# Attention units in pairs, a wider weight decode and a new order of steps in a fused attention and MoE kernel

## The chip, the cores and the metric

One core of a Trainium2 chip runs the whole program. The metric is the device time of one execution in microseconds. Before the change it is 528.5 us, the median of three runs (527.78 to 528.66).

## The reference

Three stages follow each other, all in float32, with 1,152 tokens (2 batches of 576) and 8 heads of 64:

```python
scores = q @ k.T / 8                      # windowed: heads 0-3 plain (32 keys back),
scores = where(mask, scores, -1e9)        # heads 4-7 dilated (every 4th of 128 keys back)
attn = exp(scores - max); attn /= sum + 1e-9
x = (attn @ v)                            # as 1152 x 512
h = x @ w_in                              # 512 -> 1024, w_in in float64
solu = h * softmax(h)
ln = (solu - mean) / sqrt(var + 1e-6) * g_ln
x = ln @ w_out                            # 1024 -> 512, w_out in float64
for e in range(4):                        # all four experts, weighted
    out += p[:, e] * (relu(x @ w1[e]) @ w2[e])
```

## The kernel before

Attention is cut into twelve **units**: per batch three plain ones, P0 to P2 (192 queries of four heads), and three dilated ones, D0 to D2 (96 queries per head and phase). A unit (`att_U`) goes through the engines in this way. On TensorE (PE) a mask and 24 small matmuls write its scores (L266, L275) to a PSUM tile `pa`. VectorE (DVE) takes the maximum, subtracts it, and after the exp on ScalarE (ACT) takes the sum and its reciprocal (L296 to L305). A multiply by it (L307) runs on DVE or GpSimd (POOL). Then the unit is transposed, on PE with a copy to `pt` (L326), or, for the five units in `ASWAP`, by a DVE transposition and a way through DRAM (L312 to L320). PE multiplies with V (L337), and the result is split into a high part `xhi` and the rest `xlo` (L250).

All matmuls of the dense stages use a split of this kind: three matmuls (high x high, high x low, low x high) for one product. `conv_in` and `conv_out` decode the float64 weights with integer work on the raw words: two ACT instructions (L190, L192), a shift (L194), an "or" (L196) and an add (L198) on DVE or POOL, then the split into `wh` and `wl`. w_in comes in four tiles j=0 to 3 (VI), w_out in eight halves of 512 columns (VO.j.t).

`moe_H` multiplies a tile of 128 tokens with w_in (H.0 to H.8): 24 matmuls in blocks of six, one block for each j. Blocks 0 and 1 read the plain heads, 2 and 3 the dilated ones. It writes one of two PSUM buffers `pm`; then DVE takes the maximum (L372), ACT the exp, DVE the product with `e` (L376), and ACT or DVE normalises (L379, L381). `moe_T` brings a tile into transposed form `hh`, `hl`: T.0 to T.2 on PE, T.3 to T.8 through DRAM (a DVE transposition L414, a DMA to `dt` L422, one back to `et` L431). `moe_X` multiplies three columns of 384 tokens with w_out (X.c.0 and X.c.1, 48 matmuls each, L449), also into `pm`, and copies the result to `xf`. The expert stage follows with products in Strassen form (`up`, L562) and `down` (L634).

Schedule: the instructions of every engine run in the order in which the program issues them, and that order stands in the string `ORDER`. Each word runs a generator one step further, up to its next `yield`: `UP.0.0` is a step of unit P0 of batch 0, `H.1` one of `moe_H(1)`, `VO.1.0` one of `conv_out(1, 0)`. A word that begins with `l` issues a load on SyncE's (SP) DMA queue, `F.n` runs n warm-up matmuls on a constant (L86), and a `+` at the end moves the step's flexible instruction to another engine (`pick`, `copy`):

```python
for name in ORDER.split():
    alt[0] = name.endswith("+")
    if part[0] in single:
        single[part[0]](*args)
    else:
        gens.setdefault(name, makers[part[0]](*args)); next(gens[name], None)
```

## Time and profile before

| | us |
|---|---|
| median of three runs | 528.5 |
| the profiled execution's own time | 528.32 |
| its span, first to last instruction | 526.5 |
| PE busy | 513.6 (98%) |
| DVE busy | 356.4 (68%) |
| ACT busy | 190.6 (36%) |
| POOL busy | 186.7 (35%) |

Durations come from this one execution. A matmul's end is modelled, so PE's busy time is an upper bound on its work; where PE is shown as idle, it was. The chain that ended last is PE for 90% of the span. The instructions of one engine overlap a little at their ends, so the distance between two starts is shorter than the duration of one.

### The profile page before, as it was taken

Reading aid. Unit: us, or ns where it says so; the run is one execution under the profiler, and the core shown is the slowest. Engines: PE = TensorE matmul, PEld = TensorE weight load, DVE = VectorE, ACT = ScalarE, POOL = GpSimd, SP = SyncE. Lnnn points to the kernel's source line nnn. Section 1 sums busy time; section 2 is a strip of 40 time slices with the busy share of each in tenths; the row PEclk is TensorE's granted clock in tenths of the full one; section 3 lists DMA queues with packets and bytes.
Section 4 is the critical chain, followed back from the end, with each engine's and each line's share of the span. In section 5 each row is a group of like instructions: output and inputs, shape, how many; then the busy total and the mean of one; then the engine's idle time right before and its main releaser. Section 6 shows DMA issues by size and latency. Waiting matters only on the chain.

```text
span 526.5 us, 9419 instructions
## 1 busy us (share of the span) xinstructions
PE 513.6 (98%) x3971; PEld 457.9 (87%) x3971; DVE 356.4 (68%) x474; ACT 190.6 (36%) x294; POOL 186.7 (35%) x131
## 2 busy tenths in 40 slices
PE   7789999998999999999999999999999999999997
PEld 3568889888999999998989899898989989898986
DVE  7999898484999875754775485568448655853532
ACT  3766884363153422421422233142223213312200
POOL 3334321111345632830661273047117313820300
PEclk9999999999999999999999999999999999999999
...
GB/s 321 409 319 149 146 202 78 143 159 200 1 225 95 1 1 50 111 1 1 159 1 1 8 153 0 2 153 7 2 0 161 1 0 81 0 1 1 1 81 100
DMA packets 24490, 46.44 MB, mean 88 GB/s; under 512 B 4480, under 2 KB 9088, under 8 KB 24064
## 3 DMA queue, kind: packets, MB, share of 16 engines
q1 hardware_dynamic: 24448, 45.84, 25.4%
...
## 4 chain that ended last, share of the span: by engine, by line
PE 90%; DMA 4%; DVE 2%; ACT 1%; issue 1%; SPq 1%; ACTq 0%
PE pa L634 19%; PE pm L634 18%; PE pm L562 17%; PE pa L562 17%; PE pm L367 9%; PE pm L449 6%; DMA draw<-in_moe_w_in_dram 2%; PE pa L337 1%; DMA dt<-st 1%; DMA et<-dt 1%; PE pa L275 1%; PE pa L398 1%; SPq L151 0%; DVE hl L436 0%; ACT eva L192 0%
## 5 line engine op out<-in xcount | busy, mean ns | idle before, releaser
L575 DVE SCALAR_TENSOR_TENSOR hl<-ct,hh 128x512 fp32r<-128x512 f32 (+1 forms) x64 | 64.1, 1018 | 32.4 <-ACT hh L573 32.4
L573 ACT ACTIVATE hh<-ct 128x512 fp32r<-128x512 f32 (+1 forms) x64 | 42.2, 682 | 50.8 <-DVE ct L605 21.3
L634 PE MATMUL pa<-wl,hh 128*128 128x512 f32 (+1 forms) x148 | 57.3, 387 | 0.0
L634 PE MATMUL pa<-wh,hh 128*128 128x512 f32 (+1 forms) x148 | 57.2, 387 | 0.0
L634 PE MATMUL pa<-wh,hl 128*128 128x512 f32 (+1 forms) x148 | 57.1, 386 | 0.0
L562 PE MATMUL pm<-xoh,hl 128*128 128x256 f32 (+1 forms) x192 | 56.8, 296 | 0.0
L562 PE MATMUL pa<-xoh,hl 128*128 128x256 f32 (+1 forms) x192 | 56.8, 296 | 0.0
L562 PE MATMUL pm<-xol,hh 128*128 128x256 f32 (+1 forms) x192 | 56.8, 296 | 0.0
L562 PE MATMUL pa<-xol,hh 128*128 128x256 f32 (+1 forms) x192 | 56.8, 296 | 0.0
L562 PE MATMUL pm<-xoh,hh 128*128 128x256 f32 (+1 forms) x192 | 56.8, 296 | 0.0
L562 PE MATMUL pa<-xoh,hh 128*128 128x256 f32 (+1 forms) x192 | 56.8, 296 | 0.0
L634 PE MATMUL pm<-wl,hh 128*128 128x512 f32 (+1 forms) x144 | 55.7, 387 | 0.0
L634 PE MATMUL pm<-wh,hh 128*128 128x512 f32 (+1 forms) x144 | 55.7, 387 | 0.0
L634 PE MATMUL pm<-wh,hl 128*128 128x512 f32 (+1 forms) x144 | 55.6, 386 | 0.0
L481 POOL TENSOR_TENSOR wl<-wl,wh 128x1024 fp32r<-128x1024 f32 x7 | 16.9, 2413 | 94.7 <-ACT wh L176 94.7
L639 DVE SCALAR_TENSOR_TENSOR xf<-pm,pr,xf 128x512 f32<-128x512 f32 (+1 forms) x32 | 23.6, 738 | 31.1 <-PE pm L634 31.1
L639 DVE SCALAR_TENSOR_TENSOR xf<-pa,pr,xf 128x512 f32<-128x512 f32 (+1 forms) x32 | 23.6, 738 | 30.3 <-PE pa L634 30.3
L589 POOL TENSOR_TENSOR ct<-ct,ct 128x512 f32<-128x512 f32 (+1 forms) x16 | 24.1, 1506 | 54.3 <-ACT ct L587 54.3
L176 ACT CAST wh<-wl 128x1024 fp32r<-128x1024 f32 x16 | 16.8, 1052 | 70.3 <-PE pa L634 39.8
L481 POOL TENSOR_TENSOR hl<-sw,hh 128x512 fp32r<-128x512 f32 x20 | 29.4, 1475 | 28.2 <-ACT hh L176 28.2
L562 PEld LDWEIGHTS pm<-xoh,hh 128*128 128x128 f32 x192 | 36.4, 190 | 0.3
L562 PEld LDWEIGHTS pm<-xol,hh 128*128 128x128 f32 x192 | 36.4, 190 | 0.3
...
## 6 DMA issues: line engine op xcount, KB each, us to landing
wl<-in_moe_w_dram SPq DMA_DIRECT2D x16, 512.0 KB, 4.3
cvr<-in_moe_w_out_dram SPq DMA_DIRECT2D x8, 512.0 KB, 3.5
rw<-in_moe_w_dram SPq DMA_DIRECT2D x8, 512.0 KB, 4.9
wh<-in_moe_w_dram SPq DMA_DIRECT2D x8, 512.0 KB, 6.5
...
dt<-st SPq DMA_DIRECT2D x5, 512.0 KB, 3.0
...
```

Source lines behind the costliest of these rows:

```text
L176: nc.scalar.copy(out, in_)
L275: nc.tensor.matmul(ps[32 * g:32 * g + 32, j, 64 * m:64 * m + 64], lhsT=qt[rows, h, xq:xq + 32], rhs=kt[rows, h, xq:xq + 64], start=False, ...
L337: nc.tensor.matmul(po[64 * (g % 2):64 * (g % 2) + 64, j, o:o + 32], lhsT=vt[rows, m, g, :], rhs=pt[rows, m, g, :], start=True, stop=True)
L367: nc.tensor.matmul(pm[:, n, :], lhsT=xx[:, kk, cols], rhs=ww["in", kk][:, 512 * n:512 * n + 512], start=(n_ == 0 and i < 2), stop=(n_ == K ...
L449: nc.tensor.matmul(pm[:, dd, 0:CW], lhsT=w_, rhs=x_[:, f, :], start=(f == 0 and i == 0), stop=(f == KF - 1 and i == 2))
L481: pick().tensor_tensor(out=out, in0=a, in1=b, op=op)
L562: nc.tensor.matmul(ps[:, ff, 0:n], lhsT=a[:, kk, fc], rhs=b[:, kk, :], start=kk == 0 and m == 0, stop=kk == 1 and m == 2)
L573: nc.scalar.activation(out=hv, in_=src, func=AF.Relu)
L575: nc.vector.scalar_tensor_tensor(out=lv, in0=src, scalar=0.0, in1=hv.bitcast(F32), op0=ALU.max, op1=ALU.subtract)
L589: poolv().tensor_tensor(out=c12, in0=c21, in1=c22, op=ALU.add)
L634: nc.tensor.matmul(po[:, 0, 0:dn], lhsT=h_[:, f, cols], rhs=w_, start=(f == 0 and i == 0), stop=(f == 3 and i == 2))
L639: nc.vector.scalar_tensor_tensor(out=acc[:, t, dc], in0=po[:, 0, 0:dn], scalar=pr[:, t, e:e + 1], in1=acc[:, t, dc], op0=ALU.mult, op1=ALU ...
```

## The change

Batch 0 now has four attention units, `U.0.0` = P0, `U.1.0` = D0 and D1, `U.2.0` = P1, `U.3.0` = P2 and D2; batch 1 has three pairs. The units of a pair share the PSUM tiles, one maximum, subtraction, exp, sum, reciprocal, multiply and transposition copy. The multiply works in place in the `sm` tile, of which two (for four single units) take the place of three `sm` and three `pd` tiles. A POOL memset writes the constant 1e-9 that enters the sum. Two pairs of batch 1 (D0 and D1; P2 and D2) go through DRAM. `conv_out` decodes 1,024 columns at a time. `ORDER` is new from the first word up to the first steps of the expert stage; the loop over the experts behind it is as before.

```diff
-ASWAP = ("UD.0.1", "UD.1.1", "UD.2.1", "UP.1.1", "UP.2.1")
+PB = 2
+PAIRS = (((("P", 0),), (("D", 0), ("D", 1)), (("P", 1),), (("P", 2), ("D", 2))), ((("P", 0), ("P", 1)), (("D", 0), ("D", 1)), (("P", 2), ("D", 2))))
+ASWAP = ((1, 1), (2, 1))
 ORDER = """
-F.3 lP.0.0+ UP.0.0 lI.4 VI.4+ lD.0.0 VI.4 F.1 UP.0.0+ UP.0.0 lD.1.0+ VI.4 F.1 lP.1.0+ UD.0.0 UD.1.0 UP.0.0 VI.4 lI.0 UP.0.0+ VI.4 VI.0 lP.2.0 UD.0.0 UD.0.0+
...
+lD.0.0 lP.0.0+ F.10 lD.1.0+ F.4 lP.1.0+ U.0.0 lI.4 U.1.0 lP.2.0 U.0.0+ U.0.0 U.0.0 U.1.0 U.0.0+ U.2.0 lD.2.0+ U.0.0+ U.1.0 U.0.0+ F.1 U.1.0+ VI.4+ U.2.0 U.1.0+
...
-    pds = [ap1.tile([128, 3, 128], F32, name=f"pd{i}", tag=f"pd{i}") for i in range(3)]
-    sms = [ap1.tile([128, 6, 65], F32, name=f"sm{i}", tag=f"sm{i}") for i in range(3)]
+    sms = [ap1.tile([128, 6, 130], F32, name=f"sm{i}", tag=f"sm{i}") for i in range(PB)]
...
-    def conv_out(j, t):
-        sl = slice(512 * t, 512 * t + 512)
-        a = cva[:, sl]
-        yield from convert(cvr[:, 1024 * t:1024 * t + 1024], a)
...
+    def conv_out(j):
+        yield from convert(cvr, cva)
...
+        for t in range(2):
+            sl = slice(512 * t, 512 * t + 512)
+            hi, lo = whi["out", j][:, sl], wlo["out", j][:, sl]
+            gs = g_sb[:, 2 * j + t:2 * j + t + 1]
+            nc.scalar.activation(out=hi, in_=cva[:, sl], func=AF.Copy, scale=gs)
+            yield
+            nc.vector.scalar_tensor_tensor(out=lo, in0=cva[:, sl], scalar=gs, in1=hi.bitcast(F32), op0=ALU.mult, op1=ALU.subtract)
+            yield
...
+    def att_U(k, b):
+        us = PAIRS[b][k]
+        nu, n = len(us), sum(len(PAIRS[x]) for x in range(b)) + k
+        h0 = halves[k, b]
         ps = ptile(False)
...
+        nc_ = 3 * nu
+        swap = (k, b) in ASWAP
+        sb = sms[h0 // 2 % PB][:, 3 * (h0 % 2):3 * (h0 % 2) + nc_]
+        smx = sb.rearrange("p c (j k) -> p (c j) k", j=2)
...
+        nc.gpsimd.memset(sb[:, :, 65:66] if swap else sb[:, :, 129:130], 1e-9)
+        st = small.tile([128, 3, 12], F32, name="st", tag="st")[:, :, 0:2 * nc_]
+        sv = ps[:, :, 0:192 * nu].rearrange("p j (c k) -> p j c k", k=64)
+        nc.vector.tensor_reduce(out=st[:, 0].rearrange("p (j c) -> p j c", j=2), in_=sv, axis=AX.X, op=ALU.max)
+        yield
+        nc.vector.tensor_tensor(out=sm.rearrange("p c j k -> p j c k"), in0=sv,
+                                in1=st[:, 0].rearrange("p (j c) -> p j c", j=2).unsqueeze(3).to_broadcast([128, 2, nc_, 64]), op=ALU.subtract)
+        yield
+        se = smx[:, :, 1:65] if swap else sb[:, :, 1:129]
+        nc.scalar.activation(out=se, in_=se, func=AF.Exp, scale=SCALE)
+        yield
+        nc.vector.tensor_reduce(out=st[:, 1], in_=smx, axis=AX.X, op=ALU.add)
+        yield
+        nc.vector.reciprocal(out=st[:, 2], in_=st[:, 1])
+        yield
+        pick().tensor_tensor(out=sm, in0=sm, in1=st[:, 2].rearrange("p (c j) -> p c j", j=2).unsqueeze(3).to_broadcast([128, nc_, 2, 64]), op=ALU.mult)
+        yield
...
```

How the queues move, at three places.

DVE from the first scores on (`pa` holds scores, `sm` the softmax tile, `cva` the weight under decode). Before:

```order
L296 TENSOR_REDUCE st<-pa 128x6 [waits PE_49]
L298 TENSOR_TENSOR sm_131<-pa,st 128x6x64 [waits DVE_49]
L194 TENSOR_SCALAR cva<-cva 128x512 [waits Activation_49]
L196 SCALAR_TENSOR_TENSOR cva<-draw_196,cva 128x512 [waits DMAHW1_49,DVE_49]
L303 TENSOR_REDUCE st<-sm_131 128x6 [waits Activation_49]
L198 ISA cva<-draw_196,cva 128x1024 [waits DVE_49]
L296 TENSOR_REDUCE st<-pa 128x6 [waits PE_49]
```

And now:

```order
L292 TENSOR_REDUCE st<-pa 128x6 [waits PE_49]
L294 TENSOR_TENSOR sm_128<-pa,st 128x2x3x64 [waits DVE_49]
L300 TENSOR_REDUCE st<-sm_128 128x6 [waits Activation_49,Pool_49]
L302 RECIPROCAL st<-st 128x6 [waits DVE_49]
L292 TENSOR_REDUCE st<-pa 128x12 [waits PE_49]
L294 TENSOR_TENSOR sm_129<-pa,st 128x2x6x64 [waits DVE_49]
L292 TENSOR_REDUCE st<-pa 128x6 [waits PE_49]
L294 TENSOR_TENSOR sm_128<-pa,st 128x2x3x64 [waits DVE_49,PE_49,Pool_49]
L190 TENSOR_SCALAR cva<-cva 128x512 [waits Activation_49]
```

The sum of P0 now stands directly behind its subtraction, the pair D0 and D1 has one maximum of twelve columns, and the decode of w_in comes behind three units.

PE around the first block of H.0 (`wh_198`, `wh_302` are the high part of w_in's first tile). Before:

```order
L337 MATMUL pa<-pt,vp 64x32 [waits DMAHW2_49,Activation_49]
L337 MATMUL pa<-pt,vp 64x32 x23
L337 MATMUL pa<-pt,vd_117 64x32 [waits DMAHW3_49,Activation_49]
L337 MATMUL pa<-pt,vd_117 64x32 x23
L326 MATMUL pa<-ident,pd_128 128x128 [waits DVE_49,Pool_49]
L326 MATMUL pa<-ident,pd_128 128x128 x2
L367 MATMUL pm<-wh_198,xhi 128x512 [waits Activation_49]
```

And now:

```order
L278 MATMUL pa<-qkP_120 32x64 [waits DMAHW7_49]
L278 MATMUL pa<-qkP_120 32x64 x23
L372 MATMUL pm<-wh_302,xhi 128x512 [waits Activation_49]
L372 MATMUL pm<-wh_302,xhi 128x512
L372 MATMUL pm<-wl_303,xhi 128x512 [waits Pool_49]
L372 MATMUL pm<-wl_303,xhi 128x512 [waits DVE_49]
L372 MATMUL pm<-wh_302,xlo 128x512 x2
L323 MATMUL pa<-ident,sm_128 128x128 [waits DVE_49,PE_49]
```

The scores of the first two units of batch 1 (`qkP_120` is P1's) now stand ahead of H.0, and the block waits for POOL and DVE inside.

PE where X.0 ends (L449, L454) and the next H tile begins; the number at `pm` tells the tiles apart. Before, `pm_1370` is X.0.0 (X.0.1 was `pm_1345`) and `pm_1520` H.6:

```order
L449 MATMUL pm_1370<-hl_966,wh7_1424 128x384
L449 MATMUL pm_1370<-hh_965,wl7_1425 128x384
L367 MATMUL pm_1520<-wh0_198,xhi_90 128x512 [waits DVE_49,Activation_49]
L367 MATMUL pm_1520<-wh0_198,xhi_90 128x512
L367 MATMUL pm_1520<-wl0_199,xhi_90 128x512 x2
```

Now `pm_1364` is X.0.1 (X.0.0 is `pm_1415`) and `pm_1512` H.8:

```order
L454 MATMUL pm_1364<-hl_1007,wh7_1409 128x384
L454 MATMUL pm_1364<-hh_1006,wl7_1410 128x384
L372 MATMUL pm_1512<-wh0_302,xhi_90 128x512 [waits Activation_49]
L372 MATMUL pm_1512<-wh0_302,xhi_90 128x512
L372 MATMUL pm_1512<-wl0_303,xhi_90 128x512 x2
```

H.6 and H.7 have moved ahead of X.0, H.8 stands behind it, and of the two X.0 tiles the one that was begun first is now finished last.

## Rows read from the trace of the kernel before

**Rows 1.** Windows by stage: length, busy us (instructions) of each engine, PE clock, DMA.
```profile
0.00:40.50 40.50, 32.91 (x812) 21.47 (x812) 34.94 (x74) 24.56 (x39) 14.91 (x23) 1.00 0.89 341
...
44.70:111.60 66.90, 66.90 (x732) 57.97 (x730) 54.36 (x87) 44.63 (x71) 16.80 (x13) 1.00 0.49 151
111.60:131.00 19.40, 17.36 (x99) 16.62 (x97) 11.68 (x19) 8.00 (x13) 2.61 (x2) 1.00 0.60 179
...
165.00:522.00 357.00, 357.00 (x2079) 323.43 (x2078) 218.35 (x251) 98.70 (x151) 135.47 (x84) 1.00 0.12 40
```

**Rows 2.** Timeline of PE, waits behind the dense stretch: start, us, instruction, [idle before, releaser].
```profile
112.44 0.44 PE L449 MATMUL pm<-hl,wh 128*128 128x384 f32 x1 [0.65 <-POOL hl L436]
...
130.99 0.45 PE L449 MATMUL pm<-hl,wh 128*128 128x384 f32 x1 [0.80 <-DVE hl L436]
```

**Rows 3.** Chain that ended last: start, us; an X tile and twelve H blocks.
```profile
86.74 8.52 PE pm L449 x48
95.26 16.38 PE pm L367 x72
```

**Rows 4.** Timeline of DVE, two dense neighbours of 384 elements.
```profile
30.80 0.55 DVE L303 TENSOR_REDUCE st<-sm 128x6 f32<-128x390 f32 x1
31.27 0.55 DVE L296 TENSOR_REDUCE st<-pa 128x6 f32<-128x384 f32 x1
```

**Rows 5.** Groups by form, DVE, 0 to 45 us: busy us, mean ns, idle before.
```profile
L296 DVE TENSOR_REDUCE st<-pa 128x6 f32<-128x384 f32 x10 | 5.5, 552 | 1.6 <-PE pa L275 1.5
...
L194 DVE TENSOR_SCALAR eva<-eva 128x1024 uint32<-128x1024 uint32 x2 | 1.4, 688 | 0.2 <-ACT eva L192 0.2
...
L372 DVE TENSOR_REDUCE nmx<-pm 128x1 f32<-128x1024 f32 x1 | 1.2, 1224 | 0.3 <-PE pm L367 0.3
```

**Rows 6.** Timeline of PE: warm-ups (L86) and the first scores.
```profile
1.44 1.46 PE L86 MATMUL pm<-warm 128*128 128x512 bf16 x3 [1.44 <-DVE warm L81]
...
3.97 0.97 PE L275 MATMUL pa<-qkP 64*32 64x64 f32 x48
...
15.53 1.04 PE L86 MATMUL pm<-warm 128*128 128x512 bf16 x4
```

**Rows 7.** Timeline of DVE: first and last of five idle spots, 5 to 40 us.
```profile
6.39 0.43 DVE L194 TENSOR_SCALAR cva<-cva 128x512 uint32<-128x512 uint32 x1 [0.26 <-ACT cva L192]
...
28.59 0.69 DVE L194 TENSOR_SCALAR eva<-eva 128x1024 uint32<-128x1024 uint32 x1 [0.16 <-ACT eva L192]
```

**Rows 8.** Timeline of SP's DMA queue: issue of the 25th load.
```profile
27.84 0.33 SPq L151 DMA_DIRECT2D qkD<-in_qkd_dram  x1
```

**Rows 9.** Timeline of PE: the H block behind PE's last gap of the lead-in.
```profile
40.49 0.73 PE L367 MATMUL pm<-wh,xhi 128*128 128x512 f32 x2
```

**Rows 10.** Groups by form, ACT, 0 to 150 us: the copy of an X tile.
```profile
L176 ACT COPY xf<-pm 128x768 f32<-128x768 f32 x4 | 3.2, 801 | 18.0 <-PE pm L449 18.0
```

**Rows 11.** Timeline of DVE, ACT and SP: normalising on DVE; then the way of H.7.
```profile
104.54 0.75 DVE L381 TENSOR_SCALAR e<-e,nsum 128x1024 f32<-128x1024 f32 x1
...
111.66 1.23 DVE L372 TENSOR_REDUCE nmx<-pm 128x1 f32<-128x1024 f32 x1 [1.42 <-PE pm L367]
...
115.48 1.16 ACT L379 ACTIVATE e<-e,nsum 128x1024 f32<-128x1024 f32 x1 [0.26 <-DVE e L376]
...
117.23 1.24 DVE L414 STREAM_TRANSPOSE st<-e 128x1024 f32<-128x1024 f32 x1
...
118.62 0.60 SPq L422 DMA_DIRECT2D dt<-st  x1
```

**Rows 12.** Timeline of DVE and POOL: the add of half a tile, alone and beside POOL.
```profile
7.93 0.68 DVE L198 CUSTOM_DVE_ANT_0 cva<-draw,cva 128x1024 uint16<-128x1024 uint16 x1
...
82.72 1.68 DVE L198 CUSTOM_DVE_ANT_0 cva<-cvr,cva 128x1024 uint16<-128x1024 uint16 x1
...
82.21 1.64 POOL L198 TENSOR_TENSOR cva<-cva,cvr 128x512 uint32<-128x512 uint32 x1 [7.48 <-DVE cva L196]
```

**Rows 13.** DMA issues: KB each, median us to landing.
```profile
dt<-st SPq DMA_DIRECT2D x5, 512.0 KB, 3.0
```

More of the change, by code (lines that the diff above doesn't have):

```diff
@@ L324, in att_U @@
             tp = ptile(False)
-            for m in range(3):
-                nc.tensor.transpose(tp[:, 0, 128 * m:128 * m + 128], pd[:, m, :], ident)
+            for m in range(nc_):
+                o = 128 * (m % 3)
+                nc.tensor.transpose(tp[:, m // 3, o:o + 128], sb[:, m, 1:129], ident)
             yield
-            pt = ap2.tile([128, 3, 4, 32], F32, name="pt", tag="pt")
-            copy(pt.rearrange("p m g i -> p (m g i)"), tp[:, 0, 0:384])
+            pt = ap2.tile([128, 768], F32, name="pt", tag="pt")[:, 0:384 * nu].rearrange("p (m g i) -> p m g i", g=4, i=32)
@@ L330, in att_U @@
+            copy(pt.rearrange("p (u m) g i -> p u (m g i)", u=nu), tp[:, 0:nu, 0:384])
             yield
         po = ptile(False)
-        vt = vdt[b][t] if quad == "D" else vps.pop((t, b))
-        for m in range(3):
-            for g in range(4):
-                for j in range(2):
-                    rows, o = slice(64 * j, 64 * j + 64), 96 * (g // 2) + 32 * m
-                    nc.tensor.matmul(po[64 * (g % 2):64 * (g % 2) + 64, j, o:o + 32], lhsT=vt[rows, m, g, :], rhs=pt[rows, m, g, :],
-                                     start=True, stop=True)
@@ L339, in att_U @@
-        yield
-        segs = []
-        if quad == "P":
-            s0 = b * S + TH * t
-            segs.append((xhi[:, 0:2, s0:s0 + TH], xlo[:, 0:2, s0:s0 + TH], po[:, :, 0:TH]))
-        else:
-            ov = po[:, :, 0:TH].rearrange("p j (h x) -> p h j x", h=2)
-            x = 96 * t
-            while x < 96 * t + 96:
+        tP, tD = ([t for quad, t in us if quad == q] for q in "PD")
+        dc = 192 * len(tP)
+        for ui, (quad, t) in enumerate(us):
+            vt = vdt[b][t] if quad == "D" else vps.pop((t, b))
+            for m in range(3):
+                for g in range(4):
+                    if quad == "D":
+                        o = dc + 96 * len(tD) * (g // 2) + 96 * tD.index(t) + 32 * m
+                    else:
+                        o = 192 * tP.index(t) + 96 * (g // 2) + 32 * m
+                    for j in range(2):
+                        rows = slice(64 * j, 64 * j + 64)
+                        nc.tensor.matmul(po[64 * (g % 2):64 * (g % 2) + 64, j, o:o + 32], lhsT=vt[rows, m, g, :], rhs=pt[rows, 3 * ui + m, g, :],
+                                         start=True, stop=True)
+            yield
@@ L348, in att_U @@
+        segs = []
+        if tP:
+            s0, e0 = b * S + TH * tP[0], b * S + TH * (tP[-1] + 1)
+            segs.append((xhi[:, 0:2, s0:e0], xlo[:, 0:2, s0:e0], po[:, :, 0:dc]))
+        if tD:
+            ov = po[:, :, dc:dc + 192 * len(tD)].rearrange("p j (h x) -> p h j x", h=2)
+            x0, x1 = 96 * tD[0], 96 * (tD[-1] + 1)
+            x = x0
+            while x < x1:
                 r, i = divmod(x, 144)
[L349 to L350 removed]
@@ L351, in att_U @@
-                segs.append((hv, lv, ov[:, :, :, x - 96 * t:x - 96 * t + n]))
-                x += n
+                w = min(144 - i, x1 - x)
+                hv, lv = (z[:, 2:4, b * S:b * S + S].rearrange("p h (i r j) -> p h r j i", r=2, j=2)[:, :, r, :, i:i + w] for z in (xhi, xlo))
+                segs.append((hv, lv, ov[:, :, :, x - x0:x - x0 + w]))
+                x += w
         for hv, lv, pv in segs:
```

146 lines of the change are left out of this document (54 added, 92 removed).

## The prediction

> **What bounds the kernel now.** I read the stages first, then who waits in each, then the prices. The windows by stage [rows 1] show four different kernels. From 165 to 522 us TensorE (PE) is busy for all of 357 us: 68% of the span, untouched by the change, since its matmuls and their order stay. From 44.7 to 111.6 us PE is also busy throughout, but VectorE (DVE) is busy 54.36 of 66.9 us, so the cover is thin. From 111.6 to 131 us PE is idle 19.40 - 17.36 = 2.04 us; the waits there [rows 2] name a GpSimd (POOL) and a DVE write of `hl`: the tails of T.5 and T.7, which go through DRAM. In the lead-in, up to 40.5 us, PE is idle 7.6 us and part of its "busy" is warm-up; DVE is busy 34.9 of 40.5 there and sets the pace. So the change can win or lose in three places only: the lead-in, the dense stretch (by opening a gap), and the 2 us behind it. [...]
>
> **PE's own work hardly changes.** Three transposes come (four units go through DRAM instead of five), three warm-ups go. An X tile takes 8.52 us and a block of six H matmuls 16.38/12 = 1.365 [rows 3]; their number is the same.
>
> **The lead-in, where DVE is the path.** Merging two units keeps the elements and drops instructions. On DVE, 384-element instructions start 0.47 us apart [rows 4], 0.08 less than their 0.552; 1,024 elements give 1.224 - 0.08 = 1.14 [rows 5]. The line through both is 0.07 us per instruction plus 1.047 us per 1,000 elements, so a merged instruction of 768 costs 0.87, where two cost 0.94. Five pairs with four such mergers each save 20 x 0.07 = 1.4 us of DVE time in all. The multiply by 1/sum takes that back: DVE did it for one unit (0.47), now for three pairs (2.6), the rest stays on POOL: +2.1. DVE therefore gains nothing; only the order can.
>
> [...]
>
> Now the new order. It puts 14 warm-ups ahead of the first scores, where three stood. The first three took 1.46 us, four later ones 1.04 [rows 6]; so 14 take between 14 x 0.26 = 3.6 and 14 x 0.49 = 6.8 us from 1.44. The scores of P0 (0.97 and some 0.3 for the mask) then end between 6.3 and 9.5; I take 8.0, nearer the slow row because that row is the same place in the program. Before, DVE's first maximum stood at 4.98.
>
> From that maximum to the `wl` of j=2, on which the third block of H.0 waits, the new DVE queue has 42 instructions. Ten have 384 elements, nine 768; xlo of D0 and D1 comes in two pieces (768 together), and there are five "or" (4,096), three adds (3,072) and three `wl` (2,560): 21,248 elements in 32 instructions, 22.2 + 2.2 = 24.4 us. Five shifts (4,096 elements, 0.6 us per 1,024 by [rows 5]) are 2.4, four reciprocals and a cast 0.8: together 27.6. DVE sat idle five times, 1.5 us in all, in the same stretch before (first and last in [rows 7]); the new order has as many such spots (behind exp of P0, behind the abs of j=0), so I add 1.6. Result: 8.0 + 27.6 + 1.6 = 37.2; with a hand-over to PE and a few tenths for POOL running beside it, 37.8. The loads don't bind: j=2 is the 17th load, 9.27 MB into the queue. Eight load semaphores go round, so the issue of the 25th load before, at 27.84 [rows 8], dates the landing of its 17th, with 9.4 MB. ScalarE comes to j=2 at about 28: by the same adding up, its work on j=3 gets its buffer from DVE at 25.4, and three ScalarE jobs of together 2.6 us stand before j=2. Slack: a few tenths.
>
> Compare states. Before, PE had its last gap ahead of 40.49 us [rows 9], with ten units scored, five transposed, five multiplied with V and five H blocks done. After, at 37.8, ten are scored, six transposed, five multiplied and three H blocks done. Two blocks, 2.7 us, bring it level at 40.5. **Lead-in: 0.0 us.** The bounds 6.3 and 9.5 for the start give -1.7 and +1.5; a start without slack in the loads is the first rival.
>
> **The dense stretch.** H.(t+2) reuses the PSUM buffer of H.t once DVE's product with `e` is done. From the maximum of H.0 to the product of H.2 the new DVE queue holds 24 instructions: 16,896 elements in 21 of them, 17.7 + 1.5, and a shift, two reciprocals and three reads of the accumulator, 1.0: 20.2 us. PE has from H.0's end to H.4's start H.2 and H.3 (10.9), two blocks of H.1 (2.7), two scores, five products with V and nine transposes with T.0's (7.5): 21.1 us of its own. Enough by 0.9 us: no term, but thin.
>
> One new wait is certain. X.0.1 takes the first `pm` buffer, X.0.0 the second; now X.0.1 *ends* last and H.8, which takes X.0.1's buffer, stands directly behind it. It must wait for the copy of X.0.1 to `xf`, 0.801 us on ScalarE [rows 10] plus a hand-over: **+0.9 us.** Before, the end of X.0.0 stood between.
>
> **Behind it.** The last tile's way through DRAM is covered by X.1.0 and X.1.1, 17.0 us. Before, from H.7's end at 111.64 to X.2.0 at 130.99, it took 19.35 us: maximum, exp, product, normalising on ScalarE (1.16), 0.6 us until DVE was free, transposition, two DMA hops [rows 11]. For H.8 the normalising goes to DVE (0.75, same rows) and the transposition follows at once: -0.4 and -0.6, so 18.35 us; the hops stay as they were. X.2.0 comes **1.0 us sooner** after the last H tile, and 1.35 us of idle PE remain. The first product of the Strassen stage now stands between X.2.0 and X.2.1; its operands need only X.0, X.1 and the first w1 tiles and have the 8.5 us of X.2.0: nothing. The w_out decode in whole tiles keeps its elements and halves its instructions, inside the dense stretch: nothing, as long as DVE isn't the bound there.
>
> **Sum.** 0.0 + 0.9 - 1.0 = -0.1 us on the profiled execution's 528.32 us (span 526.5 and 1.8 around it), which is 0.2 below the median of 528.5: 528.2 us. About 0.2%, 1.06 us, is what a measurement of this kernel can tell from no change.
>
> **Rivals.**
> - *DVE's chain starts early.* If the 14 warm-ups run at the fast price, P0's scores end near 6.3 and everything up to H.0's third block comes up to 1.7 us sooner; with another 0.2 from spots where DVE idles less, 526.3 us. For it: only D0 and P0 are loaded ahead, and PE has no gap between the warm-ups. Against it: the slow row at the same place, and a load of j=2 with tenths of slack.
> - *DVE becomes the bound in the dense stretch: slower.* The place is H.2 to X.0. Once DVE is over 0.9 us behind between H.0 and H.4, each further loss delays an H tile and PE idles where it never did. Price: the add of half a w_out tile took 1.68 us beside a POOL instruction of 1.64, where the same shape took 0.68 without [rows 12]. POOL now adds whole tiles, some 2.5 us each, beside DVE multiplies that were POOL's; three such meetings cost 3.0 us, less the slack of 0.9: +2.1, 530.3 us. Against it: one such meeting in twelve conversions before. [...]
> - *The mergers do less than they say.* If 768 elements in the new split layout cost 0.95 instead of 0.87, nine in the lead-in add 0.7 us: 528.9. That stays inside the forecast's range and has no chance of its own.
>
> **How the numbers follow.** The forecast, three terms that cancel: 0.41, with a range of its own from 527.3 to 529.4. An early chain: 0.33, since half of its gain already passes 1.06 us. DVE-bound: 0.26. These three are same, faster and slower. As the signs differ, the range reaches to both rivals: downward to 526.3 less 0.6, as the DMA hop of 512 KB that took 5.6 us in the chain has a median of 3.0 [rows 13] and could give up to the remaining 1.35; upward to 530.3 and 0.7 for half of the late start: 525.7 to 531.0.
>
> **What would show it.** Right: the first maximum on DVE near 8 us; the third block of H.0 near 37.8; PE without a gap from there until a wait of 0.9 us on ScalarE ahead of H.8; about 1.3 us of idle PE ahead of X.2.0; from there to the end the same length as before. Wrong: a first maximum before 6.8 us with H.0's third block before 36.5 (first rival); PE waiting on DVE in front of H.2 to H.7 or X.0 (second); or a stretch after X.2.0 that differs by more than 0.3 us, for which nothing here speaks.

## The result and the profile after

The changed kernel takes **532.7 us** (median of four runs, 531.99 to 532.98), the kernel before 528.58 in the same session (527.78 to 528.97): a ratio of 1.0078, 95% interval [1.006, 1.0095], 4.1 us slower. The forecast was 528.2 in a range from 525.7 to 531.0. It is wrong in size and in direction. The profiled execution has a span of 530.6 us, 4.1 more than before.

The windows of the kernel after; the stages are cut as in [rows 1], moved by what each one starts later (columns as there):

```profile
0.00:40.50 40.50, 30.89 (x804) 20.66 (x807) 32.86 (x57) 21.76 (x27) 11.90 (x25) 0.92 0.95 360
46.40:115.60 69.20, 67.55 (x607) 57.55 (x595) 57.34 (x76) 43.38 (x63) 9.74 (x5) 1.00 0.42 137
115.60:134.00 18.40, 17.27 (x98) 16.75 (x98) 12.88 (x18) 5.56 (x8) 4.83 (x2) 1.00 0.60 166
169.00:526.00 357.00, 356.55 (x2075) 322.74 (x2074) 217.09 (x253) 97.05 (x149) 132.77 (x83) 1.00 0.12 40
```

PE, idle 7.6 us in the first 40.5 before, is idle 9.6 now, and its granted clock is 0.92 there. The dense stretch has 1.65 us of gaps where there was none. The 2.04 us of idle PE behind it have become 1.13. The 357 us of the expert stage have a gap of 0.45 at their start. The longer waits of PE, from its timeline (start, us, instruction, [idle before, releaser]):

```profile
1.45 4.59 PE L83 MATMUL pm<-warm 128*128 128x512 bf16 x14 [1.45 <-DVE warm L78]
...
13.29 0.60 PE L83 MATMUL pm<-warm 128*128 128x512 bf16 x2 [0.86 <-issue]
16.97 0.84 PE L323 MATMUL pa<-ident,sm 128*128 128x128 f32 x6 [1.33 <-DVE sm L304]
...
25.68 0.21 PE L341 MATMUL pa<-pt,vd 64*64 64x32 f32 x1 [4.25 <-issue]
...
50.51 0.72 PE L372 MATMUL pm<-wh,xhi 128*128 128x512 f32 x2 [0.36 <-DVE e L381]
86.26 0.70 PE L372 MATMUL pm<-wh,xhi 128*128 128x512 f32 x2 [0.40 <-DVE e L381]
109.91 0.74 PE L372 MATMUL pm<-wh,xhi 128*128 128x512 f32 x2 [0.89 <-ACT xf L172]
116.83 0.41 PE L454 MATMUL pm<-hl,wh 128*128 128x384 f32 x1 [0.85 <-DVE hl L441]
134.01 0.41 PE L454 MATMUL pm<-hl,wh 128*128 128x384 f32 x1 [0.29 <-DVE hl L441]
...
174.17 0.50 PE L639 MATMUL pa<-wh,hh 128*128 128x512 f32 x1 [0.45 <-DVE ct L598]
```

Against [rows 2] the waits ahead of X.1.0 and X.2.0 are 0.85 + 0.29 where they were 0.65 + 0.59 + 0.80. New are the 0.89 ahead of H.8, the two waits for DVE's product with `e` and a stop of 4.25 us with no releaser at all, which the trace calls "issue". DVE's queue in the lead-in, from its first maximum to that of H.0, from the timeline of DVE:

```profile
6.90 0.56 DVE L292 TENSOR_REDUCE st<-pa 128x6 f32<-128x384 f32 x1 [2.28 <-PE pa L278]
7.49 0.56 DVE L294 TENSOR_TENSOR sm<-pa,st 128x384 f32<-128x384 f32 x1
...
34.03 1.22 DVE L192 SCALAR_TENSOR_TENSOR cva<-draw,cva 128x1024 uint32<-128x1024 uint32 x1
35.28 1.23 DVE L194 CUSTOM_DVE_ANT_0 cva<-draw,cva 128x2048 uint16<-128x2048 uint16 x1
36.43 0.55 DVE L246 TENSOR_TENSOR xlo<-pa,xhi 128x384 fp32r<-128x384 f32 x1
36.90 1.22 DVE L194 CUSTOM_DVE_ANT_0 eva<-draw,eva 128x2048 uint16<-128x2048 uint16 x1
38.03 1.22 DVE L221 TENSOR_TENSOR wl<-cva,wh 128x1024 fp32r<-128x1024 f32 x1
...
43.88 1.23 DVE L377 TENSOR_REDUCE nmx<-pm 128x1 f32<-128x1024 f32 x1 [0.34 <-PE pm L372]
```

The same two ends in the kernel before, from its timeline of DVE:

```profile
4.98 0.56 DVE L296 TENSOR_REDUCE st<-pa 128x6 f32<-128x384 f32 x1 [0.55 <-PE pa L275]
...
42.18 1.22 DVE L372 TENSOR_REDUCE nmx<-pm 128x1 f32<-128x1024 f32 x1 [0.28 <-PE pm L367]
```

From its first maximum to that of H.0 DVE needs 36.98 us now and needed 37.20 before. It starts 1.92 us later and arrives 1.70 later. From there to X.1.0 PE has the same matmuls in both kernels. So the 4.1 us are made up of: 1.70 at H.0's maximum; 0.36 + 0.40 for DVE in front of H tiles; 0.89 ahead of H.8; 1.14 - 2.04 = -0.90 ahead of X.1.0 and X.2.0; and, from X.2.0's last wait (134.01 against 130.99) to the end, 1.1. That is 3.5; the other 0.6 stand in none of these waits and were not followed up.

What held PE in the changed lead-in is read from its own rows behind the long stop, and from POOL's row for the memset behind its multiply of U.3.0:

```profile
33.17 0.87 PE L323 MATMUL pa<-ident,sm 128*128 128x128 f32 x6
...
35.03 0.33 PE L269 MATMUL pa<-mask,identb 128*128 128x192 bf16 x2 [0.16 <-ACT pt L172]
...
39.46 0.73 PE L372 MATMUL pm<-wh,xhi 128*128 128x512 f32 x2
40.03 0.62 PE L372 MATMUL pm<-wl,xhi 128*128 128x512 f32 x2
```

```profile
33.05 0.11 POOL L289 MEMSET sm<- 128x6 f32 x1
```

From 25.68 to H.0's third block at 39.46, PE has one gap, of 0.16 us. DVE's `wl` for this block ended at 39.25, and PE read it at 40.03, 0.78 us later: at its end DVE's queue is not what PE waits for. The place where the two meet lies before it, at the transposition of U.3.0. POOL was done with its part at 33.16, behind DVE's reciprocal at 31.24; PE, late from its stop and the granted clock of 0.50 behind it, from 24.8 to 31.6 us, came at 33.17. From there on it is PE's own work, with one copy of ACT: 10.7 us to H.0's maximum.

### The profile page after: what moved, and what is told of

The parts are those of the page before. It is cut to its first block, busy times and chain, and to the rows that moved or that the text cites. A ratio compares the mean times of both kernels' runs of the same rounds, so it can differ in the third digit from the quotient of the medians.

```text
span 530.6 us, 9337 instructions
## 1 busy us (share of the span) xinstructions
PE 514.4 (97%) x3971; PEld 458.0 (86%) x3974; DVE 356.8 (67%) x443; ACT 187.7 (35%) x274; POOL 180.7 (34%) x127
## 4 chain that ended last, share of the span: by engine, by line
PE 86%; DVE 7%; DMA 2%; issue 2%; ACT 2%; SPq 0%; DVEq 0%
PE pa L639 18%; PE pm L639 18%; PE pm L567 15%; PE pa L567 15%; PE pm L372 8%; PE pm L454 6%; PE pa L341 2%; DMA et<-dt 1%; PE pm L83 1%; DMA dt<-st 1%; PE pa L278 1%; DVE hl L441 1%; DVE xol L486 1%; PE pa L403 1%; DVE st L300 1%
## 5 line engine op out<-in xcount | busy, mean ns | idle before, releaser
L580 DVE SCALAR_TENSOR_TENSOR hl<-ct,hh 128x512 fp32r<-128x512 f32 (+1 forms) x64 | 61.8, 983 | 34.0 <-ACT hh L578 34.0
L644 DVE SCALAR_TENSOR_TENSOR xf<-pa,pr,xf 128x512 f32<-128x512 f32 (+1 forms) x32 | 23.6, 738 | 30.4 <-PE pa L639 30.4
L486 POOL TENSOR_TENSOR hl<-sw,hh 128x512 fp32r<-128x512 f32 x21 | 31.3, 1493 | 27.6 <-ACT hh L172 25.3
```

Source lines behind the costliest of these rows:

```text
L486: pick().tensor_tensor(out=out, in0=a, in1=b, op=op)
L580: nc.vector.scalar_tensor_tensor(out=lv, in0=src, scalar=0.0, in1=hv.bitcast(F32), op0=ALU.max, op1=ALU.subtract)
L644: nc.vector.scalar_tensor_tensor(out=acc[:, t, dc], in0=po[:, 0, 0:dn], scalar=pr[:, t, e:e + 1], in1=acc[:, t, dc], op0=ALU.mult, op1=ALU ...
```

## The experiments

Ratios are to the kernel before, with their 95% interval. Three questions: what the parts behind the lead-in cost, what holds the lead-in, and whether its start alone does. Each trace is of one execution, so a kernel's trace can lie off its median.

**e1_tail.** The order of the kernel before, from X.1.1 on.

```diff
-endH XQ.0 X.1.1+ X.1.1+ lW.0 X.2.0 WP.0+ XQ.0+ XQ.0 WP.0 ...
+endH XQ.0 X.1.1+ X.1.1+ X.2.0 XQ.0 XQ.0 lW.0 WP.0+ WP.0 X.2.1+ ...
```

> The changed kernel, with the order of before from X.2 on (its instructions are the same, only their order behind X.1.1 changes). The changed kernel was 4.1 us slower by its profile: 3.0 at the start of X.2.0 (134.01 against 130.99) and a further 1.1 to 1.2 until the first run of up products behind the first down tiles. Theory: this last piece belongs to the new order of the first expert steps, in which PE waits for DVE in front of two products (0.18 and 0.45 us). Then this kernel is some 1.1 us faster than the changed one, ratio to before 1.0057. Rival: DVE arrives late there anyway, because X.2 does; then the piece stays, ratio 1.0078.

Measured: 532.54 us, 1.0068 [1.0045, 1.0091]. The times of the changed kernel and of this one overlap, but the traces tell the part: from X.2.0's last wait to the end it takes 530.3 - 134.70 = 395.6 us, the changed kernel 530.6 - 134.01 = 396.6, the kernel before 526.5 - 130.99 = 395.5; the waits for `ct` at 159 and 174 us are gone. Between these two traces the new order of the first expert steps costs 1.0 us. It does not always: e4, e9, e11 and e13 below keep the new order and have no wait for `ct`. From X.1.0's last wait to the end they take 412.0 to 412.1 us, this kernel 412.75 and the changed kernel 413.8. What brings the waits about was not found.

**e2_xswap.** X.0.0 ends last again, as before the change.

```diff
-T.3+ X.0.0+ T.6 X.0.1+ H.7+ X.0.1
+T.3+ X.0.1+ T.6 X.0.0+ H.7+ X.0.1
```

> The changed kernel, with the second halves of X.0.0 and X.0.1 exchanged, so that X.0.1 ends first and its buffer is copied while X.0.0 runs. The wait of 0.89 us on ScalarE ahead of H.8 goes in every theory. Theory: behind H.8 the start of X.1.0 hangs on T.5, whose load from DRAM waits for T.3's buffer, which waits for the end of X.0; so X.1.0 stays at 116.8 us and only the 0.29 us ahead of X.2.0 are won: ratio 1.0073. Rival: PE is the path there, the whole 0.9 us is won: ratio 1.0061.

Measured: 534.28 us, 1.0102 [1.0077, 1.0128]. H.8 no longer waits, but nothing is won. The timeline of PE, and the windows behind it (columns as above):

```profile
117.49 0.41 PE L454 MATMUL pm<-hh,wh 128*128 128x384 f32 x1 [1.19 <-DVE hh L170]
118.75 0.41 PE L454 MATMUL pm<-hl,wh 128*128 128x384 f32 x1 [0.85 <-DVE hl L441]
```

```profile
112.00:119.30 7.30, 5.26 (x23) 3.96 (x22) 4.58 (x5) 3.73 (x7) 3.04 (x1) 1.00 0.74 214
119.30:122.70 3.40, 3.40 (x13) 3.40 (x12) 2.09 (x4) 2.14 (x3) 0.00 (x0) 0.51 0.68 158
```

The 0.89 us only went on to X.1.0, whose operand from T.5 comes no sooner: from H.0's maximum to X.1.0's last wait it takes 73.1 us, in the changed kernel 72.95. Behind the 2.04 us of idle time PE's granted clock was 0.51 for 3.4 us; neither theory had that. The larger part of this trace's delay is older: its warm-ups took 5.73 us instead of 4.59, and H.0's maximum came 1.81 us later.

**e3_et3.** The same, with a third `et` buffer and T.5's two steps ahead of X.0.0's end.

```diff
-T.3+ X.0.1+ T.6 X.0.0+ H.7+ X.0.1 T.4 T.6 T.5 T.3+ T.4+ T.3 X.0.0 T.5+ T.6
+T.3+ X.0.1+ T.5 T.5+ T.6 X.0.0+ H.7+ X.0.1 T.4 T.6 T.3+ T.4+ T.3 X.0.0 T.6
-name=f"et{t % 2}", tag=f"et{t % 2}"
+name=f"et{t % 3}", tag=f"et{t % 3}"
```

> As the kernel with the exchanged halves of X.0, and a third et buffer, so that T.5's load from DRAM no longer waits for T.3. Theory of T.5's buffer: the wait of 0.85 us inside X.1.0 goes too, X.1.0 starts near 114.7 us, and X.2.0 is then set by H.8's way through DRAM (18.35 us behind H.8's end, so near 133.0): 1.0 us faster than the changed kernel, ratio 1.0059. Rival: the wait inside X.1.0 has another cause (POOL's hl of T.4); then as the kernel before in this list, ratio 1.0061 to 1.0073.

Measured: 532.3 us, 1.0063 [1.0038, 1.0088]. The waits from H.8 to X.2.0 are down from 2.03 to 0.57 us; the time does not differ from the changed kernel's beyond its interval. X.1.0 hung on T.5's way through DRAM; the buffer and the earlier steps were changed together and not told apart.

**e8_before2.** The kernel before, with its own waits of [rows 2] taken away: `hl` of T.5 on DVE, H.7 normalised on DVE and transposed at once (as the change does for H.8), a second buffer `st4`, T.7's transfer ahead of T.8's.

```diff
-H.8+ T.5+ H.8+ H.7 X.1.0 ... T.8+ H.7 T.6+ T.8+ T.6 H.7+ T.8+ X.1.0+ T.7+ T.8+ X.1.1 X.1.1+ T.7+ T.8 T.7+ sc T.7
+H.8+ T.5 H.8+ H.7 X.1.0 ... T.8+ H.7 H.7 T.7+ T.7+ T.6+ T.8+ T.6 T.7+ sc T.8+ X.1.0+ T.8+ X.1.1 X.1.1+ T.8 T.7
-name="st4", tag="st4"
+name=f"st4{t % 2}", tag=f"st4{t % 2}"
```

> The kernel before, with the one part of the change that the profile shows to be worth something, and its two waits behind the dense stretch: H.7 is normalised on DVE and transposed directly behind (the last tile's way took 18.35 us in the changed kernel, 19.35 before), with a second st4 buffer so that T.7 needn't wait for T.8's transfer, T.5's hl on DVE instead of GpSimd, T.7's transfer ahead of T.8's on the queue. Theory: the wait of 0.65 us ahead of X.1.0 goes, X.2.0 starts near 130.0 instead of 131.0 us, the kernel is 1.0 us faster, ratio 0.998. Rival: T.8's transfer, now later, ends last, and X.2.0 stays at 131: ratio 1.000.

Measured: **526.14 us, 0.995 [0.9926, 0.9975]**: faster than either kernel, and by more than the 1.0 us expected. Its window, against the third of [rows 1] with 17.36 us of busy PE:

```profile
111.60:131.00 19.40, 19.26 (x111) 18.94 (x110) 14.69 (x22) 7.25 (x12) 2.72 (x2) 1.00 0.63 180
```

So the place where the change was to win does hold 2 us, and they can be had without it.

**e12_back.** The changed kernel with e1's and e3's edits together; its lead-in is untouched.

> The changed kernel with its lead-in as it is, and everything behind it mended: halves of X.0 exchanged, a third et buffer, T.5's load earlier, the order of before behind X.1.1. Theory that the loss behind the lead-in is 0.9 (wait ahead of H.8) and 1.0 (expert start), less 1.1 for the last tile's way: 2.0 us faster than the changed kernel, ratio 1.004; what is left, some 2 us, is the lead-in. If the parts are not separate: as the changed kernel less 1.0, 1.006.

Measured: 532.11 us, 1.0055 [1.0033, 1.0076], though its first maximum happened to stand at 8.47 us, 1.57 later than in the changed kernel's trace. Of the 3.7 us that this trace is longer than that of the kernel before, 3.26 stand at H.0's maximum: what is left is mostly the lead-in.

**e4_warm3.** Three warm-ups ahead of the first scores in place of 14 (`F.10 lD.1.0+ F.4` becomes `F.3 lD.1.0+`).

> The changed kernel, with 3 of the 14 warm-up matmuls in front left (22 PE instructions fewer, counting weight loads). The changed kernel's PE stood still from 21.43 to 25.68 us with nothing to wait for, behind its 959th instruction; its shorter stops without a releaser came behind the 448th and 703rd, always 256 apart. Theory: PE gets its instructions in blocks of 256 through the same DMA rings as the loads; the stop stays behind the 959th instruction, which is now 11 matmuls further on in the program, inside the scores of U.0.1, and it comes and ends earlier, by 1 to 1.6 us; the clock falls less or not. By that the kernel gains 0 to 2 us (ratio 1.004 to 1.0078), more if PE's lateness is the path, nothing if DVE's chain is. Rival: PE waited there for something of the data (a load, a buffer); then the stop stays ahead of the last product of U.1.0 with V at about 21.4 to 25.7 us.

Measured: 531.85 us, 1.0056 [1.0034, 1.0077]. The first maximum came at 6.32 only, since P0 is the second load. PE's long stop shrank from 4.25 to 1.49 us, and yet H.0's maximum came at 44.12, 0.24 later than in the changed kernel: PE now waited for DVE (1.77 us ahead of the scores of U.0.1) and for POOL (0.87 ahead of U.3.0's transposition). The shorter time comes from behind the lead-in: 412.1 us from X.1.0's last wait to the end instead of 413.8 (see e1).

**e5_relief14.** The lead-in's DVE queue relieved: a copy and a split go to ACT and an add to POOL, another add comes to DVE, and U.3.0's reciprocal and multiply stand directly behind its sum.

```diff
-VI.1 VI.0 U.0.0+ VI.1 VI.0 U.1.0+ VI.1 VI.3 ... VI.0+ lI.2+ VI.0 VI.1 U.3.0+ VI.4 VI.0+ VI.3+ VI.0 lD.0.1+ VI.0+
+VI.1 VI.0 VI.1+ VI.0 U.0.0 U.1.0+ VI.3 ... VI.0+ lI.2+ VI.0 VI.0 VI.0 VI.1 U.3.0+ U.3.0 VI.4 VI.1 lD.0.1+ VI.0+ U.3.0+
...
```

> The changed kernel, with work taken out of DVE's queue in the lead-in, all 14 front warm-ups kept: the copy of U.0.0's transposition and its xhi go to ScalarE, the add of w_in's second tile to GpSimd, the add of the first tile's second half comes to DVE (it took 2.16 us on GpSimd and held up ScalarE's xhi of U.1.0), U.3.0's reciprocal and multiply come directly behind its sum. By the durations in the trace of the changed kernel the maximum of U.0.1 starts on DVE at 30.0 instead of 31.4 us and wl of tile 2 ends at 37.9 instead of 39.25. Theory that PE's instruction supply also binds (the stop to 25.7 us, behind which PE has work without a gap): little is won, 0 to 0.5 us, ratio 1.0070 to 1.0078. Theory that DVE's chain alone binds: 1.1 to 1.4 us are won, ratio 1.0052 to 1.0057.

Measured: 536.67 us, 1.0141 [1.0113, 1.017]: 4 us worse than the changed kernel. In its trace H.0's maximum comes 3.16 us later; 1.47 of that is a later first maximum (8.37), as its warm-ups took 6.06 us. DVE, then POOL, in its timelines:

```profile
22.79 2.04 DVE L190 TENSOR_SCALAR cva<-cva 128x512 uint32<-128x512 uint32 x1
...
28.76 2.49 DVE L221 TENSOR_TENSOR wl<-eva,wh 128x1024 fp32r<-128x1024 f32 x1
...
22.15 2.40 POOL L194 TENSOR_TENSOR eva<-eva,draw 128x1024 uint32<-128x1024 uint32 x1 [2.38 <-ACT cva L188]
...
28.25 1.93 POOL L304 TENSOR_TENSOR sm<-sm,st 128x768 f32<-128x768 f32 x1
```

The shift that takes 0.42 us alone took 2.04, the `wl` of 1.22 took 2.49, and they ended 0.28 and 1.07 us behind POOL's instruction beside them, which had begun first. So here, where DVE was to be relieved, two of its instructions took 1.62 and 1.27 us longer beside POOL's; by which mechanism was not shown.

**e6_relief3, e7_all.** e5's edit with three warm-ups; and that together with e12's edits.

> The same relief of DVE, with 3 of the 14 front warm-ups. With 3 warm-ups alone the kernel stood at ratio 1.0056, its PE waited 0.87 us for GpSimd's multiply of U.3.0 at 33.4 us. Theory that both bind, PE's supply and DVE's chain: this is the kernel in which both are relieved, the third block of H.0 comes near 38.6 instead of 39.7 us, 1.1 us faster than with 3 warm-ups alone, ratio 1.0035. Rival, that PE's own work behind 25.8 us (at half clock until 29.7) binds: as with 3 warm-ups alone, 1.0056.

> The changed kernel with everything together: the relief of DVE and 3 warm-ups in front, the halves of X.0 exchanged and a third et buffer, the order of before behind X.1.1. If the four losses are separate and add up (4.1 us by the profile: lead-in, the wait ahead of H.8, the expert start, less the shorter way of the last tile), the kernel comes to 532.7 - 2.2 (lead-in) - 1.0 (X.0 and et) - 1.0 (expert start) = 528.5 us, ratio 1.000. If the gains ahead of X.1.0 only move PE's waits to X.1.0 and X.2.0, it stays near 529.7, ratio 1.0023.

Measured: 536.09 us, 1.0122 [1.0096, 1.0148], and 533.42, 1.0086 [1.0057, 1.0116]. DVE's way from the first maximum to H.0's grew to 41.22 and 40.32 us, and the mean granted clock of the profiled run was 0.984 and 0.983, against 0.993 in the changed kernel: 48 score matmuls took 0.97 us at 27.47 in e6 and at 26.90 in e7, and 0.73 at 39.16 and 38.31. Both expectations missed. The two stretched instructions of e5 stand in these traces too (2.04 and 2.06 us, 2.49 in both); what they cost and what the clock cost was not told apart.

**e9_skip, e10_noadd, e11_both.** PE has a third fewer score matmuls in batch 0 (`for m in (0, 2) if b == 0 else range(3)`); DVE and POOL don't add the low words of w_in's tiles 1 to 3; and both.

> The changed kernel, leaving out a third of the score matmuls of batch 0 (32 PE instructions of each unit, 192 in all, 1.4 us of PE's work in the lead-in); nothing else moves. This relieves PE's instruction supply alone: the stop behind the 959th instruction falls 192 instructions later in the program, behind nearly all scores of U.0.1, which then run before it, at about 23 to 25 us instead of 25.8 to 28.5. Theory that the supply (and the half clock behind its stop) sets the lead-in: H.0's third block comes 1 to 2.5 us before the 39.5 us of the changed kernel, ratio 1.003 to 1.006. Theory that DVE's chain sets it: the third block stays within 0.4 us, PE waits ahead of the transposition of U.3.0 near 33 us, ratio 1.007 to 1.0078.

> The changed kernel, leaving out the add of the low words of w_in's tiles 1, 2 and 3 (three DVE instructions of 1.15 us each; one lies before the maximum of U.0.1, all three before wl of tile 2). This relieves DVE's chain alone, without moving work to GpSimd. Theory that DVE's chain sets the lead-in: H.0's third block comes 1.1 to 3.4 us sooner, ratio 1.0015 to 1.0057. Theory that PE's supply and its work behind the stop set it: 0 to 0.5 us, ratio 1.007 to 1.0078, and DVE waits where it did not.

> Both at once: a third of the score matmuls of batch 0 and the three adds left out. If the two bind side by side, this one gains clearly more than the two alone together: 2 to 3.5 us in the lead-in, ratio 1.001 to 1.004. If DVE's chain alone binds, it is as with the adds left out alone; if the supply alone, as with the score matmuls left out alone.

Measured: 533.41 us, 1.0081 [1.0055, 1.0107]; 533.14, 1.0074 [1.0045, 1.0104]; 533.17, 1.0084 [1.0053, 1.0115]. None wins. In e9 the stop of 4.25 us is replaced by two of 2.71 and 2.50, so PE's supply was not relieved. In e10 DVE is done with the `wl` that H.0's third block needs 29.7 us behind its first maximum, 2.64 sooner than in the changed kernel, but H.0's maximum comes only 1.1 sooner (35.85 instead of 36.98): PE reads this `wl` 2.29 us after it is done, and DVE waits 1.68 us for PE. The 1.1 us themselves can't be put down to DVE alone. POOL was ready for U.3.0's transposition 1.02 us sooner behind the first maximum, but PE came 0.98 us sooner as well, since the full clock was back 22.8 us behind the first maximum instead of 24.7. So two limits meet at this transposition in the changed lead-in: the chain from DVE to POOL, and PE with its stop and its lower clock. Over the traces either comes first:

```profile
34.72 0.88 PE L323 MATMUL pa<-ident,sm 128*128 128x128 f32 x6 [0.57 <-POOL sm L289]
```

```profile
35.23 0.82 PE L323 MATMUL pa<-ident,sm 128*128 128x128 f32 x6
```

The first row is e12's: PE waits 0.57 us for POOL, and in e4, e14 and e16 0.87. The second is e2's: POOL had been ready at 34.31, 0.92 us before PE came; in e1 and e3 it was 0.54 and 0.31. From the transposition to H.0's maximum it takes 10.46 to 10.73 us in all these kernels, in e10, e13 and in the changed one, and in each of them the `wl` is done at least 0.77 us before PE reads it. The traces also showed what I had not yet allowed for: e10's warm-ups took 6.02 us, so that its first maximum was late, at 8.34.

**e13_early, e14_early_back.** The changed kernel, and e12, with the start of the kernel before: P0's load first, three warm-ups.

```diff
-lD.0.0 lP.0.0+ F.10 lD.1.0+ F.4 lP.1.0+ U.0.0
+lP.0.0+ lD.0.0 F.3 lD.1.0+ lP.1.0+ U.0.0
```

> The changed kernel with the first two loads exchanged (P0's q and k ahead of D0's) and 3 warm-ups ahead of the first scores where 14 stood, as in the kernel before; nothing else. First maximum expected at about 5.0 us instead of 6.9. Theory A (the late start carries the lead-in loss: everything that follows hangs on VectorE's chain from the first maximum): H.0's third block comes near 37.6 instead of 39.5, the start of X.1.0 1.9 us sooner, 530.8 us. Theory B (TensorE's instruction blocks of 256 arrive no faster than the loads let them, and the clock halves behind each stop): the stop behind the 959th instruction grows by what the start wins, H.0's third block stays within 0.5 us of 39.5, 532.2 us or more.

> e13_early together with the repairs of e12_back (second halves of X.0 exchanged, third et buffer, the order of the kernel before behind X.1.1). Theory A: 532.1 - 1.9 = 530.2 us. Theory B: 532.1 within 0.5 us. If both are partly right, 531.

Measured: 531.73 us, 1.0055 [1.0037, 1.0073], and 530.37, 1.0025 [1.0006, 1.0044]. By its time e14 lies with theory A (1.7 us below e12) and e13 between the two. The traces don't bear theory A out. In e13 H.0's third block came at 40.98, 1.5 us later than in the changed kernel, where 37.6 was expected; what its trace wins stands behind X.1.0, from whose last wait it takes 412.05 us to the end instead of 413.8 (see e1). In e14 H.0's maximum came 0.12 us before the changed kernel's. PE's and DVE's rows in e14:

```profile
8.05 0.97 PE L278 MATMUL pa<-qkD 64*32 64x64 f32 x48 [1.17 <-DMA qkD<-in_qkd_dram]
```

```profile
5.16 0.56 DVE L292 TENSOR_REDUCE st<-pa 128x6 f32<-128x384 f32 x1 [0.55 <-PE pa L278]
...
9.06 0.96 DVE L292 TENSOR_REDUCE st<-pa 128x12 f32<-128x768 f32 x1 [1.29 <-PE pa L278]
...
12.23 0.56 DVE L294 TENSOR_TENSOR sm<-pa,st 128x384 f32<-128x384 f32 x1 [0.76 <-PE pa L323]
...
43.76 1.22 DVE L377 TENSOR_REDUCE nmx<-pm 128x1 f32<-128x1024 f32 x1 [0.35 <-PE pm L372]
```

The early start is lost again within 7 us: the pair D0 and D1 now waits for its load, with no decode of w_in to fill the gap as before. From 12.2 us on the queue stands where it stood in the changed kernel. Compared with the kernel before, H.0's maximum is 1.58 us late and the span 527.9 - 526.5 = 1.4 longer: with the repairs behind it, nothing but the lead-in is left.

**e15_late.** The kernel before, with the start of the changed one and nothing else.

```diff
-F.3 lP.0.0+ UP.0.0 lI.4 VI.4+ lD.0.0 VI.4 F.1
+lD.0.0 lP.0.0+ F.10 F.4 UP.0.0 lI.4 VI.4+ VI.4 F.1
```

> The kernel BEFORE with only the start of the changed one: D0's load ahead of P0's and 14 warm-ups ahead of the first scores where 3 stood. First maximum expected near 6.9 instead of 4.98. Theory A: every later milestone of the lead-in 1.9 us later, PE's last gap of the lead-in ends at 42.4 instead of 40.5, 530.5 us (ratio 1.0036). Theory B: before's chain has no such stop, its PE has 7.6 us of idle time in the lead-in that takes the delay only where VectorE does not set the pace; it gives a loss below 0.5 us, and 528.6 to 529.1 us.

Measured: 531.5 us, 1.0057 [1.0038, 1.0075]. First and last row of DVE's chain:

```profile
7.10 0.56 DVE L296 TENSOR_REDUCE st<-pa 128x6 f32<-128x384 f32 x1 [2.67 <-PE pa L275]
...
43.65 1.23 DVE L372 TENSOR_REDUCE nmx<-pm 128x1 f32<-128x1024 f32 x1 [0.25 <-PE pm L367]
```

2.12 us later at the first maximum, 1.47 at H.0's, 1.65 at X.2.0 (132.64 against 130.99), and 1.7 in the span of this execution (528.2). Its time, 529.99, is one of the shortest of twelve (529.91 to 533.86); the median loses 3.0 us, which this trace does not show. The way from the first to H.0's maximum is 0.65 us shorter than before, so PE's 7.6 us of idle time absorb at most that much of the 2.12. Theory A holds in the main: the late start by itself, load order and warm-ups together, makes the kernel before slower.

**e16_later.** The changed kernel with eight more warm-ups (`F.10` becomes `F.18`).

> The changed kernel with 22 warm-ups ahead of the first scores where 14 stood; nothing else. The eight more take 2.1 to 2.6 us (0.26 to 0.33 each). In eight traces with either lead-in VectorE's way from its first maximum to the maximum of H.0 took 36.6 to 37.7 us, wherever the first one stood. Theory A (that way is rigid, so the start sets the lead-in): first maximum 2.1 to 2.6 us later than in a changed kernel of the same clock rise (near 9 to 10 us), H.0's maximum 37 us behind it, 534.9 us. Theory B (TensorE's stops or the loads set the lead-in): the delay vanishes in TensorE's idle time, the way from the first to H.0's maximum shrinks to 35, 532.7 to 533.2 us.

Measured: 537.41 us, 1.0149 [1.0118, 1.018]: 4.7 us above the changed kernel. The first maximum stood at 9.31, 2.41 later, H.0's at 48.61, 4.73 later. The rest is in two rows, of PE and of DVE:

```profile
15.40 0.96 PE L83 MATMUL pm<-warm 128*128 128x512 bf16 x3 [3.04 <-issue]
...
17.10 0.56 DVE L294 TENSOR_TENSOR sm<-pa,st 128x384 f32<-128x384 f32 x1 [2.89 <-PE pa L323]
```

Theory A's direction holds and theory B's absorption fails; but the price was twice what A said, because the later start moved a stop of PE onto DVE's path: behind the 3.04 us DVE waited 2.89. In the changed kernel DVE waited 0.29 us at this instruction.

DVE's way over the runs, from the timelines of DVE (us):

| kernel | first maximum | H.0's maximum | way |
|---|---|---|---|
| before | 4.98 | 42.18 | 37.20 |
| e8_before2 | 4.98 | 42.10 | 37.12 |
| e15_late | 7.10 | 43.65 | 36.55 |
| after (the changed kernel) | 6.90 | 43.88 | 36.98 |
| e1_tail | 7.33 | 44.63 | 37.30 |
| e3_et3 | 7.37 | 44.42 | 37.05 |
| e2_xswap | 8.04 | 45.69 | 37.65 |
| e12_back | 8.47 | 45.44 | 36.97 |
| e10_noadd | 8.34 | 44.19 | 35.85 |
| e14_early_back | 5.16 | 43.76 | 38.60 |
| e16_later | 9.31 | 48.61 | 39.30 |

Eight kernels with either lead-in lie within 1.1 us, with starts 3.5 us apart. They run over different instructions, and nothing in the traces ties the two sums together. The three last rows are those with less DVE work, with a wait for a load, and with a stop on the path; e4, e5, e6, e7, e9, e11 and e13, whose edits all reach into the lead-in, took 37.8 to 41.5.

## Why the prediction was wrong, point by point

- **The lead-in, forecast 0.0: wrong, +1.70 us at H.0's maximum.** Two steps of the forecast failed, and the first is the path. The prediction lets H.0's third block wait for the `wl` of j=2 at the end of DVE's queue and has no term for PE there ("PE's own work hardly changes"), neither for its stops nor for its clock. In the changed kernel this `wl` was ready 0.78 us before PE read it. What the block hung on was the transposition of U.3.0 at 33.17, where POOL behind DVE, and PE behind a stop of 4.25 us and 6.8 us of half clock, arrived together; from there PE's own work runs. The clock of 1.00 in [rows 1] hid a slow stretch before as well: 48 score matmuls took 0.97 us at 3.97 and 0.72 at 13.95.
- **The second step is the length of DVE's queue, forecast 27.6 us and 1.6 of idle spots: too short.** The start came at 6.90, earlier than my 8.0 (14 warm-ups at 0.33 us each; in other runs they took up to 6.15). From the first maximum to the end of the `wl` at 39.25 it took 32.35 us: 1.96 idle, 30.4 of work, 2.8 more than forecast, and 2.3 of it ahead of U.3.0's reciprocal. Four sizes were off. The price per instruction came from two neighbours that don't depend on each other [rows 4]; dependent ones stood further apart: "or" to add is 1.25 us apart (34.03 to 35.28) where add to an unrelated `wl` is 1.13, maximum to subtraction 0.59 where I took 0.47. The five shifts took 3.0 us, not 2.4. The two pieces of xlo of D0 and D1 took 1.53 from the first start to the next instruction's, where my line gives 0.94. And `wl` of 512 took 0.84 from start to start, not 0.61.
- **The comparison of states.** H.0's third block began at 39.46, 1.66 behind my 37.8, and H.0's maximum came 1.70 late: the two blocks that I set against the kernel before were counted rightly. What the count hid is the late start. The way from the first to H.0's maximum, about 37 us, came out as long in both kernels, so a start 1.92 us later shows as 1.70. In the kernel before, e15 shows such a price by experiment (1.47 of 2.12 us); in the changed kernel an earlier start (e13, e14) was lost to the load of D0, so there the start as the cause is argued, not shown.
- **The mergers.** Right in sign and larger than priced: a pair's maximum and subtraction stand 0.95 us apart, two single ones twice 0.59, so a merger saves 0.23 where the next instruction depends on it, not 0.07. But those savings are inside the 30.4 us above.
- **The dense stretch, forecast "enough by 0.9, no term".** The cover was thin as said, and failed twice, for 0.36 and 0.40 us in front of an H tile: 0.76. It is the place and kind of the second rival, DVE late with the product that frees an H tile's buffer, at a third of its price. Not by the meetings that it priced, though: POOL's three adds of whole tiles took 2.41 to 2.44 us there, and DVE's dense instructions beside them, which read one of their inputs from PSUM, kept their 1.2 us.
- **The wait ahead of H.8, forecast +0.9: right,** 0.89 on ACT's copy to `xf`. e2 shows that taking it away alone wins nothing.
- **The last tile's way, forecast 18.35 us: right in the sum, in part by luck.** From H.8's end at 115.68 to X.2.0's last wait at 134.01 it took 18.33. The step that I priced is as forecast: from the maximum to the transposition 4.55 us where it had been 5.57. Two others cancelled: DVE began H.8's maximum 0.9 us late (116.60), being busy with `hl` of T.5, and the hop to DRAM took, as it happens, 4.55 us where it had taken 5.57. The waits there fell by 0.90 instead of 1.0, as X.1.0's own grew from 0.65 to 0.85.
- **From X.2.0 to the end, forecast the same length: wrong, +1.1** in this trace. The waits for `ct` are new; e1 removes them with the old order, and e4, e9, e11 and e13 don't have them in the new one. I let the operands' readiness decide and didn't count DVE's queue in the first expert steps, where [rows 1] stops at 131 us and starts again at 165: I had no row of it.
- **The early-chain rival (0.33)** had the start wrong: it came at 6.90, not near 6.3, and e13 and e14 show that even a first maximum at 5.16 is lost to the load of D0.

What stays open: in the changed lead-in the chain from DVE to POOL and PE's stop with the half clock behind it meet at U.3.0's transposition within 0.01 us. e4, with the stop at 1.49 us, was held by the first, e10 doesn't tell them apart, and no run relieves both without another loss. How much of PE's part is the stops and how much the clock was not told apart either.
